# RWKV-6 recurrence and a gated Fourier convolution on one core: states by ScalarE in pieces, merged VectorE sums, a new order

## The chip, the cores and the metric

The kernel runs on one core of a Trainium2 chip. A core has TensorE (PE; its weight loads are listed as PEld), VectorE (DVE), ScalarE (ACT), GpSimd (POOL), and SyncE (SP), whose queue issues the DMAs here. The metric is the device time of one execution in microseconds (us); less is better.

## The reference

Four sequences of 768 steps pass through eight heads of 48 columns with a decaying state, and the result through a gated circular convolution along the sequence.

```python
# r, k, v, w: (4, 8, 768, 48); u: (8, 48)
for t in range(S):
    cur = einsum('bhd,bhe->bhde', u[None] * kt, vt)
    y[:, :, t] = einsum('bhd,bhde->bhe', rt, state + cur)       # the "bonus" is the part with u
    state = wt[:, :, :, None] * state + einsum('bhd,bhe->bhde', kt, vt)
x = y.transpose(0, 2, 1, 3).reshape(B, S, H * D)                # (4, 768, 384)
proj = x @ w_proj                                               # (384, 3 * 384)
x1, x2, x3 = split(proj, 3, axis=-1)
x2_conv = irfft(rfft(x2, axis=1) * rfft(filter_fft, axis=0), n=S, axis=1)
out = (x1 * x2_conv * x3) @ w_out                               # (4, 768, 384)
```

## The kernel before

**Chunks.** The sequence is cut into chunks of 128 steps: six for each of the four sequences (batches), 24 in all, numbered 0 to 23. The steps of a chunk lie on the partitions, the 8 x 48 columns beside each other. For each chunk, four loads of 192 KB (`ldw`, `ldr`, `ldk`, `ldv`, rings of six buffers) are followed by:

- the logarithm of w (`lw`, ScalarE), its running sums by matmuls with triangular masks (`cs`, `ce`), and exponentials (`en`, `eq`; `enp`, `eqp` in place in PSUM), by which k and r are scaled (`kh`, `q` on GpSimd, `khp`, `qp` on VectorE);
- transposes of q and k (`tqk`, TensorE), copied to SBUF in one piece of 128x1024 (`tT`, seen in the trace as `qkT<-tqk`), scores (`sc`), masked on VectorE (`mt`) or copied and then masked (`ma`, `mm`);
- the state: `kv` adds k'v to the last state, and `S` scales the sum by the chunk's decay and writes it as bf16. The next chunk's `kv` and its `y` need it;
- the bonus: `rk`, `rku`, a row sum `cc`, and its product with v, `vc`. Either a matmul adds it (`yb`, then the copy `xc`), or VectorE does (`y`, then `xn`);
- transposes of the chunk's output (`yt`), copied (`xT`).

**Batches.** When the chunks of a sequence are there, the convolution follows as matrix work. Sums and differences of mirrored chunks (`sa`, `sb`, then `fp`, `fm` for each of two halves q) go through the projection `x2`; copies `ab`; the Fourier matmuls `f` with six slots; products with the filter's transform (`da`, `db`, straight from PSUM) and their sums `pp` for each of three column blocks n; the inverse `i1`, `i2`, a copy `ec`, sum and difference `s`, `d`. The other two projections, `p1` (copied by `x1`) and `p3`, give the gate `g`; `yy` multiplies, `po` projects, `o` copies and `st` stores. The last batch uses half-size steps (`i1h`, `i2h`, `ech`, `sh`, `dh`, `yyh`, `poa`, `pob`). The filter's transform and the Fourier matrices (sines, `sin`) are made at the start.

**Order.** The text `ORDER` lists every operation with its engine (V, A, G, P, S for VectorE, ScalarE, GpSimd, TensorE, SyncE) and, behind @, its PSUM bank. Each engine works through its own entries strictly in that order; between engines, semaphores wait for the data and for free buffers. A GpSimd operation marked with ! also waits for the last VectorE operation ahead of it in the text that belongs to the set `shut`. So a late operation holds up everything behind it on its engine. Copies have one line in a helper (L237 on ScalarE, L238 elsewhere), and are told apart in the trace by their tiles. Rows of L464 are the loads of w, r, k, v, of L367 those of the projection weights.

Of the kernel before, what the change touches and what calls it, by code (L numbers as in the profile page):

```python
# [53 lines left out]
P:yt5@1 P:ce7@5 V:sa4 P:x20.0.1@3 V:khp6 A:xT5 A:eq7 V:sb4 P:tqk6@4 V:sa5 A:ab0.0.1 P:x20.1.1@5
V:sb5 V:fp0.0 A:xT3 S:ldr7 A:v6 V:fm0.1 P:x20.0.0@3 P:x20.1.2@2 V:rku6 V:fm0.0 V:fp0.1 S:ldw8 G:q7!
P:x20.0.2@1 S:ldk7 A:ab0.0.0 S:ldp0 A:ab0.1.2 A:ab0.1.1 V:tT6 A:ab0.0.2 S:ldw10 V:cc6 P:f0.0@3
G:kh7! A:xT4 S:ldk8 P:kv6@2 P:x20.1.0@4 V:da0.0 G:vc6! A:ab0.1.0 A:lw8 P:f0.3@1 A:hb2 V:S6 G:rk7!
P:sc6@8 S:ldr8 P:f0.2@4 P:f0.4@2 A:wc0 P:ce8@3 P:tqk7@0 A:eq8 V:db0.1 A:tT7 S:ldw9 P:f0.5@1 P:cs8@5
V:da0.1 V:da0.2 G:rku7! P:p10.2.1@4 V:mt6 G:pp0.1! P:p10.0.1@3 P:p10.2.0@2 A:x10.2.1 S:ldv7 V:db0.2
# [6 lines left out]
S:ldr10 P:p30.0.1@1 A:lw11 V:S8 V:xn8 S:ldk10 A:en10 P:yt6@4 P:ce11@2 V:d0.1 A:tT9 G:q10! S:ldr11
A:eqp11 A:xT6 S:ldw12 S:ldv9 P:p30.0.0@3 G:kh10! A:lw12 V:g0.0.1 V:cc9 V:g0.0.0 P:yt8@5 P:i10.2@0
P:cs11@1 P:sc9@8 A:xT8 A:en11 P:tqk10@4 G:rk10! V:qp11 A:v9 G:rku10! P:p30.1.0@3 S:ldk11 P:p11.0.0@1
A:tT10 P:p11.1.0@2 G:vc9! G:kh11! P:kv9@5 P:cs12@4 A:x11.0.0 V:mt9 V:g0.1.0 V:d0.2 S:ldv10 A:x11.1.0
P:ce12@3 P:y9@1 P:sc10@8 P:tqk11@2 S:ldv11 S:ldw13 A:v10 V:S9 A:eq12 S:ldr12 P:kv10@3 V:cc10 S:ldk12  # L70
# [12 lines left out]
V:da1.1 P:p31.0.1@1 P:kv13@3 P:tqk14@4 G:vc12! P:ce16@0 S:ldr19 P:yb12@2 V:g1.1.1 V:S13 S:ldk19
P:po0.2@5 P:po0.0@3 A:tT14 V:mt13 P:p31.2.1@4 G:rh14! A:xc12 A:eq16 G:vc13! P:cs16@2 P:sc14@8
P:yt12@0 S:ldv19 V:g1.0.1 V:ch14 V:g1.2.1 A:o0.2 P:yb13@5 A:v14 A:enp16 G:kh15! A:o0.0 A:xc13 V:mt14
V:khp16 G:rk15! P:f1.4@4 G:q15! A:xT12 P:tqk15@1 G:q16! G:vc14! G:rku15! G:rk16! P:yt13@5 A:tT15
P:y14@3 A:lw17 A:xT13 S:ldr21 S:ldw21 P:kv14@0 P:tqk16@2 S:ldw23 V:da1.2 V:xn14 A:tT16 P:f1.5@1
P:po0.5@4 S:ldv20 P:yt14@5 P:po0.1@3 V:S14 V:cc15 P:f1.1@0 V:db1.2 G:rk17! P:sc15@8 A:o0.5 A:xT14
# [6 lines left out]
P:i21.2@1 A:eq18 P:i21.0@0 S:st0.3 A:x12.0.0 V:mt17 V:S16 A:v18 A:lw19 G:vc15! P:yt16@3 P:yb15@4
G:q18! A:ec1.2 G:rku18! P:ce19@1 A:v17 A:ec1.0 A:xc15 S:ldv23 S:ldv22 P:tqk18@2 A:tT18 V:sa16 V:sb16
V:xT16 P:y17@0 P:i21.1@3 A:ec1.1 A:eq19 V:d1.0 V:s1.0 P:i11.2@4 G:vc17! V:xn17 P:yt15@2 P:cs19@5
P:x22.1.1@0 G:kh20! V:cc18 A:xT15 G:q20! P:yt17@1 P:i11.1@3 P:sc18@8 A:enp19 V:d1.2 V:s1.2 V:sb15
P:tqk20@4 V:sa15 A:xT17 P:p12.2.1@2 A:ab2.1.1 A:ma18 G:q19! G:rk19! P:p32.0.1@0 V:khp19 G:rk20!
V:sa17 V:d1.1 V:sb17 A:x12.2.1 A:tT20 V:s1.1 P:x22.0.1@5 P:p12.1.1@1 A:ab2.0.1 P:p32.0.0@3 V:fm2.0  # L100
# [852 lines left out]
```

## Time and profile before

| | |
|---|---|
| median of 3 runs | 151.19 us (150.94 to 152.24) |
| the profiled execution | 150.74 us |
| its span, first to last instruction | 148.9 us |
| granted TensorE clock, mean | 0.951 |
| busy, share of the span | PE 90%, DVE 91%, ACT 88%, POOL 73% |
| instructions | PE 1499, DVE 278, ACT 274, POOL 133 |
| HBM read, written | 22.41 MB, 4.72 MB |

Times within the trace count from the start of the span. 1.84 us of the profiled execution's time lie outside it. A share of busy time is a mean over the whole span; an instruction's duration overlaps with the next one's start by about 0.1 us on ScalarE and VectorE, so that the distance from start to start is shorter than the duration.

### The profile page before, as it was taken

To read this page: it belongs to the slowest core of one execution; us is meant where nothing else is said; L and a number is where in the kernel's file an instruction comes from. 1 tells how busy PE (TensorE), PEld (TensorE's weight loads), DVE (VectorE), ACT (ScalarE), POOL (GpSimd) and SP (SyncE) were. 2 spreads that over 40 slices of the span, in tenths; PEclk is the share of its full clock that TensorE was granted. 3 is DMA by queue.
4 is the path that set the end of the run, shared out by engine and by line. 5 is a ranking of instruction groups with operands and counts; after the bars stand their busy time and mean duration, and the time that the engine had idled before them with its cause. 6 is when DMAs were issued, how large, how long until landed. Compare 5 with 4: busy or idle time off the path is not lost.

```text
span 148.9 us, 4080 instructions
## 1 busy us (share of the span) xinstructions
PE 134.0 (90%) x1499; PEld 89.9 (60%) x1499; DVE 134.8 (91%) x278; ACT 130.7 (88%) x274; POOL 108.8 (73%) x133
## 2 busy tenths in 40 slices
...
GB/s 80 212 278 218 181 210 187 219 188 243 178 258 201 263 203 183 217 167 214 227 232 200 222 204 194 198 168 219 229 186 0 4 173 254 0 0 53 314 210 170
...
## 3 DMA queue, kind: packets, MB, share of 16 engines
...
q8 instruction: 11, 0.18, 0.5%
...
HBM read 22.41 MB, written 4.72 MB: 182 GB/s over the span
## 4 chain that ended last, share of the span: by engine, by line
PE 68%; DMA 12%; SPq 5%; POOL 4%; DVE 4%; issue 3%; ACT 1%; ACTq 0%; DVEq 0%; POOLq 0%
PE p L688 14%; PE po L852 8%; PE i L773 6%; PE x L719 6%; PE tqk L561 6%; DMA filt<-in_moe_filter_fft_dram 5%; SPq L464 5%; PE sc L574 4%; DMA ldv<-in_v_dram 4%; DMA ldk<-in_k_dram 3%; PE f L739 3%; PE y L627 2%; PE yt L650 2%; PE cs L474 2%; PE kv L602 2%
## 5 line engine op out<-in xcount | busy, mean ns | idle before, releaser
L535 POOL TENSOR_TENSOR rk<-ldr,ldk 128x384 bf16<-128x384 f32 x23 | 23.0, 1003 | 11.1 <-DMA ldr<-in_r_dram 5.6
L688 PE MATMUL p<-xT,wproj 128*128 128x384 bf16 x144 | 28.8, 326 | 0.0
L555 POOL TENSOR_TENSOR vc<-v,cc 128x384 bf16<-128x384 bf16 x24 | 19.9, 831 | 10.5 <-PE sc L574 3.1
L581 DVE TENSOR_TENSOR mt<-sc,mask_excl 128x1024 bf16<-128x1024 f32 x21 | 25.4, 1210 | 0.1
L237 ACT ACTIVATE qkT<-tqk 128x1024 bf16<-128x1024 bf16 x22 | 22.7, 1031 | 0.7 <-PE tqk L561 0.5
L532 POOL TENSOR_TENSOR qk<-ldr,eq 128x384 bf16<-128x384 f32 x20 | 20.1, 1007 | 3.3 <-DVE rku L538 1.8
L561 PE MATMUL tqk<-ident,qk 128*128 128x128 bf16 x192 | 16.2, 228 | 2.6 <-POOL qk L532 1.8
L688 PEld LDWEIGHTS <-wproj 128*128 128x128 bf16 x144 | 13.0, 97 | 7.4 <-ACT wproj L237 0.3
L561 PEld LDWEIGHTS <-qk 128*128 128x128 bf16 x192 | 12.7, 102 | 5.5 <-POOL qk L532 2.2
L470 ACT ACTIVATE lg<-ldw 128x384 bf16<-128x384 f32 x24 | 12.6, 532 | 2.8 <-DMA ldw<-in_w_dram 2.8
L852 PE MATMUL po<-wout,y 128*128 128x384 bf16 x72 | 14.4, 326 | 0.0
L237 ACT ACTIVATE x<-p 128x384 bf16<-128x384 f32 x24 | 11.7, 505 | 1.5 <-PE p L688 1.5
L237 ACT ACTIVATE ab<-x 128x384 bf16<-128x384 f32 x24 | 11.7, 501 | 1.1 <-PE x L719 0.8
L538 POOL TENSOR_TENSOR rku<-rk,u_bc 128x384 bf16<-128x384 bf16 x13 | 11.8, 913 | 0.4
L541 DVE TENSOR_REDUCE cc<-rku 128x8 f32<-128x384 bf16 x22 | 11.7, 537 | 0.0
L499 ACT ACTIVATE eq<-ce 128x392 f32<-128x392 f32 (+1 forms) x21 | 10.6, 514 | 0.6 <-PE ce L486 0.3
L764 DVE TENSOR_TENSOR UB<-f,T 128x768 bf16<-128x768 f32 x12 | 11.1, 943 | 0.0
L237 ACT ACTIVATE v<-ldv 128x384 bf16<-128x384 f32 x20 | 10.8, 548 | 0.3 <-DMA ldv<-in_v_dram 0.2
L237 ACT ACTIVATE xT<-yt 128x384 bf16<-128x384 bf16 x22 | 10.8, 503 | 0.2
L610 DVE TENSOR_TENSOR S<-kv,eq 128x384 bf16<-128x384 f32 x20 | 10.9, 543 | 0.0
L528 POOL TENSOR_TENSOR qk<-ldk,en 128x384 bf16<-128x384 f32 x10 | 10.0, 1003 | 0.8 <-DMA ldk<-in_k_dram 0.8
L761 DVE TENSOR_TENSOR UA<-f,T 128x768 bf16<-128x768 f32 x11 | 10.3, 943 | 0.1
...
## 6 DMA issues: line engine op xcount, KB each, us to landing
...
```

The costliest lines, as they stand in the source:

```text
L237: return nc.scalar.activation(out=o, in_=i, func=AF.Copy)
L470: nc.scalar.activation(out=lg_b[c % 3][:, :, 0:D], in_=ld["w"][c % LD], func=AF.Ln)
L532: return two(e).tensor_mul(qk_b[c % 3][:, 0, :, 0:D], ld["r"][c % LD], eq)
L535: return two(e).tensor_mul(rk_b[c % 2], ld["r"][c % LD], ld["k"][c % LD])
L538: return two(e).tensor_mul(rku_b[c % 2], rk_b[c % 2], u_bc)
L541: nc.vector.tensor_reduce(out=cc_b[c % 3], in_=rku_b[c % 2], axis=AX.X, op=ALU.add)
L555: return two(e).tensor_mul(vc_b[c % 3], v_b[c % 4], cc_b[c % 3].to_broadcast([L, H, D]))
L561: nc.tensor.transpose(p[:, x, j, :], qk_b[c % 3][:, x, 2 * j:2 * j + 2, :], ident)
L581: nc.vector.tensor_mul(mt_b[c % 3], bank_of[f"sc{c}"].rearrange("p q j t -> p (q j) t"), dataclasses.replace(m[:, :], ap=[m[:, :].ap[0], [ ...
L688: nc.tensor.matmul(p, wproj[:, n, cb, fb * L:(fb + 1) * L], xT_b[b % 2][:, NT * hf:NT * hf + NT, cb, :], start=(cb == 0), stop=(cb == CB - 1),
L764: nc.vector.tensor_mul(UB[:, n], twice(bank_of[f"f.{b}.{2 * n + 1}"][:, :]), t2(n, 1))
L852: nc.tensor.matmul(p, y_b[0][:, cb, ti * L:(ti + 1) * L], wout[:, cb, :], start=(cb == FIRST[0]), stop=(cb == FIRST[-1]),)
```

## The change

The state `S` gets a second form on ScalarE: eight activations with a scale column in place of one VectorE product. It is used for chunks 0, 4, 7, 8, 9, 10, 19, 21 and 22. The bonus products `vc` of chunks 0 and 7 move from GpSimd to VectorE, and chunks 5, 12 and 19 get `xn` on VectorE in place of the bonus matmul and the copy `xc`. The tiles of three rings become one tile each, so that one VectorE instruction does the work of two or three: `fpm`, `fmm` (both halves), `ppm` (three blocks), `yym` (three blocks). Part of the last product is cut in quarters (`yyq`). The halved row sum (`rh`, `ch`) goes. The sines are made first, in four separate steps with one table load, ahead of the table for logarithms and exponentials. `hm`, `um` and `uw` prepare a mask whose result the new order doesn't use. The whole `ORDER` is written anew: many copies and products change engine (on ScalarE fewer `v`, `xT`, `xc`; on GpSimd fewer `rku`, `pp`; on VectorE fewer `khp`, more `xT`), and the loads come in another sequence. The other new functions of the diff stand unused.

The part of `ORDER` around chunk 8, before and after:

```
-A:x10.1.0 P:sc7@8 P:ce9@5 V:db0.0 G:q8! P:tqk8@2 G:v7! V:cc7 V:pp0.0 V:pp0.2 A:eq9 P:p10.1.1@1
-P:kv7@4 P:cs9@5 A:tT8 P:i20.0@3 P:i10.0@2 V:rku8 V:mt7 S:ldp2 V:S7 A:x10.1.1 A:ec0.0 A:en9 A:x10.0.0
-S:ldr9 P:ce10@1 P:i20.2@3 A:wc2 A:ec0.2 S:ldk9 P:sc8@8 V:cc8 V:d0.0 V:s0.0 G:vc7! P:i20.1@4
...
+A:xT6 A:tT7 A:v7 V:db0.1 G:wc0! G:kh8! G:q8! P:p10.0.1@2 P:f0.1@5 A:hb2 S:ldr9 P:p10.1.0@4 P:tqk8@3
+A:x10.0.1 P:f0.4@1 P:p10.2.0@2 P:sc7@8 V:db0.0 P:kv7@5 S:ldk9 S:ldv8 S:ldp2 A:tT8 A:x10.1.0
+A:x10.2.0 G:rku7! P:ce9@3 V:da0.1 G:rk8! P:cs9@4 A:S7 V:da0.2 P:p10.1.1@1 P:p10.0.0@2 A:v8 P:ce10@5
+S:ldw11 V:cc7 P:kv8@0 V:ppm0 V:vc7 A:eq9 P:i20.1@3 V:rku8 A:en9 A:x10.0.0 A:x10.1.1 A:wc2 V:mt7
+P:i20.0@4 P:p10.2.1@2 P:yb7@1 G:kh9! A:eq10 V:x10.2.1 P:sc8@8 A:S8 G:q9! P:p30.2.0@2 A:ec0.0 S:ldw13
```

The loads at the start, and the stretch with the late states:

```
-S:ldw1 S:ldu S:ldw0 S:ldr0 S:ldk0 S:ldk1 S:ldw2 S:ldr1 S:ldfilt S:ldv0 S:ldw3 S:ldr2 ... S:ldw7 S:ldv5 S:ldp1 S:ldk6 ...
+S:ldk1 S:ldw1 S:ldu S:ldw3 S:ldw0 S:ldr1 S:ldv1 S:ldr0 S:ldw2 S:ldk0 S:ldfilt S:ldv0 ... S:ldr6 S:ldk6 S:ldp1 S:ldw7 ...
-A:xT19 A:tT23 A:v22 V:cc22 P:sc22@8 P:po1.0@2 V:mt22 P:po1.5@1 P:yt20@0 P:po1.4@4 P:kv22@5 V:da2.2
-P:sc23@8 V:S22 A:v23 A:o1.5 ...
+V:xT18 V:cc21 P:po1.5@2 P:tqk23@1 V:da2.0 A:tT23 P:sc22@8 P:f2.2@4 A:o1.5 A:xT20 G:rk23! P:kv21@3
+V:rku22 A:S21 G:rku23! V:mt22 G:v23! P:f2.4@0 P:po1.4@1 ... A:v22 P:po1.0@3 V:cc22 P:kv22@2
+V:da2.2 A:x13.1.0 A:X2.2 P:p13.0.0@5 P:y21@4 V:mt23 A:S22 A:o1.4 V:ua2.1 P:p33.0.0@0 A:o1.0 G:vc22!
+A:gc3.0.0 P:y23@2 ...
```

The code:

```diff
@@ op_S
         ph = eq_b[c % 3][:, C:].rearrange("p (a b) -> p a b", b=2)
+        if e == "A":
+            for j in range(HP):
+                for i in (0, 1):
+                    nc.scalar.activation(
+                        out=S_b[nth(c)][:, j, i], in_=bank_of[f"kv{c}"][:, j, i], func=AF.Copy,
+                        scale=ph[:, j, i:i + 1],
+                    )
+            return
         nc.vector.tensor_mul(
             S_b[nth(c)], bank_of[f"kv{c}"], ph.to_broadcast([L, HP, 2, D])
         )
@@ tiles
-    sd_b = ring("sd", 2, [L, NT, CB, L], BF16)
+    sd = consts.tile([L, 2, NT, CB, L], BF16)
-    fo_b = ring("fo", 2, [L, 2, CB, L], BF16)
+    fo = consts.tile([L, 2, 2, CB, L], BF16)
-    SD_b = ring("SD", 3, [L, S], BF16)
+    SD = consts.tile([L, CB, S], BF16)
@@ merged sums and products
+    def op_fpm(e, b):
+        return two(e).tensor_add(fo[:, :, 0], sd[:, :, 0], sd[:, :, 2])
+    def op_fmm(e, b):
+        return two(e).tensor_sub(fo[:, :, 1], sd[:, :, 0], sd[:, :, 2])
+    def op_ppm(e, b):
+        return two(e).tensor_add(P_b[b % 2], UA, UB)
+    def op_yym(e, b):
+        return two(e).tensor_mul(y_b[0], SD, g_b[b % 2])
+    def op_yyq(e, b, cb, a, pt):
+        sl = slice(HALF * a + QUART * pt, HALF * a + QUART * pt + QUART)
+        return two(e).tensor_mul(y_b[0][:, cb, sl], SD[:, cb, sl], g_b[b % 2][:, cb, sl])
@@ the sines
-    def op_sin(e, k_):
-        for ti in range(NT):
-            nc.scalar.activation(out=F[:, ti, :], ..., func=AF.Sin, ...)
-        nc.scalar.activation(out=rot, in_=rang, func=AF.Sin, scale=TWO_PI / (2 * S))
-        nc.scalar.preload_act_table_set("natural_log_exp_and_others")
+    def op_tS(e, k_):
+        nc.scalar.preload_act_table(AF.Sin)
+    def op_sn(e, ti):
+        nc.scalar.activation(out=F[:, ti, :], ..., func=AF.Sin, ...)
+    def op_sr(e, k_):
+        nc.scalar.activation(out=rot, in_=rang, func=AF.Sin, scale=TWO_PI / (2 * S))
```

More of the change, by code (lines that the diff above doesn't have):

```diff
@@ L54 @@
[L54 to L59, printed above, removed]
@@ L66 @@
[L66 to L70, printed above, removed]
@@ L83 @@
[L83 to L88, printed above, removed]
@@ L95 @@
[L95 to L100, printed above, removed]
@@ L107 @@
-P:cs23@4 A:xT18 P:tqk21@0 A:o1.2 V:xn20 V:cc21 A:en23 V:S20 P:x22.0.0@5 P:f2.1@3 G:q22! P:ce23@4
-A:tT21 G:kh22! V:db2.0 G:kh23! G:v21! A:eqp23 P:f2.5@1 V:qp23 A:ab2.0.0 V:db2.2 P:yb19@2 P:sc21@8
-A:xc19 A:ma21 P:f2.0@5 P:tqk22@2 V:da2.0 A:tT22 G:rku22! P:yt19@4 P:f2.4@3 P:kv21@1 P:tqk23@0 V:S21
-A:xT19 A:tT23 A:v22 V:cc22 P:sc22@8 P:po1.0@2 V:mt22 P:po1.5@1 P:yt20@0 P:po1.4@4 P:kv22@5 V:da2.2
-P:sc23@8 V:S22 A:v23 A:o1.5 G:vc21! G:rk23! G:rku23! G:mm21! G:pp2.2! A:xT20 A:o1.0 A:o1.4 P:f2.2@1
-P:y22@3 P:p13.1.0@5 V:mt23 A:x13.1.0 V:cc23 P:y21@4 P:p13.2.0@2 A:x13.2.0 P:p33.0.0@5 P:y23@0
@@ L113 @@
-A:gc3.0.0 G:vc23! G:vc22! P:p13.0.0@2 V:xn21 V:da2.1 P:p33.1.0@5 V:xn23 V:pp2.0 P:yt23@0 V:pp2.1
-P:yt21@1 P:p33.2.0@4 V:gm2.1.1 V:xn22 A:gc3.1.0 A:x13.0.0 A:xT23 P:i12.0@5 P:i22.2@2 V:g3.2.0 V:sb21
-A:ec2.2 P:yt22@3 V:sa21 P:i22.0@0 G:sa23! G:sb23! A:ec2.0 V:sa22 V:sb22 V:fp3.0 P:i22.1@4 V:fm3.1
-A:ec2.1 A:xT22 P:i12.2@2 P:i12.1@0 P:x23.1.2@4 P:x23.1.1@3 V:d2.2 V:s2.0 A:xT21 V:s2.1 V:d2.0
-G:gm2.2.1! G:fp3.1! P:x23.0.0@1 V:s2.2 A:ab3.1.2 P:p13.1.1@4 P:x23.1.0@5 G:fm3.0! A:ab3.0.0 V:d2.1
-V:yy2.1 P:x23.0.1@2 V:yy2.2 P:x23.0.2@0 A:ab3.1.1 A:ab3.1.0 A:ab3.0.1 V:gm2.0.1 A:ab3.0.2 V:yy2.0
@@ new lines @@
+S:ldw11 V:cc7 P:kv8@0 V:ppm0 V:vc7 A:eq9 P:i20.1@3 V:rku8 A:en9 A:x10.0.0 A:x10.1.1 A:wc2 V:mt7
+P:i20.0@4 P:p10.2.1@2 P:yb7@1 G:kh9! A:eq10 V:x10.2.1 P:sc8@8 A:S8 G:q9! P:p30.2.0@2 A:ec0.0 S:ldw13
+V:ec0.1 S:ldk10 P:i10.1@3 P:p30.1.0@0 S:ldr10 V:cc8 G:rk9! G:vc8! P:tqk9@4 V:mt8 A:lw11 P:y8@5
+S:ldv11 V:g0.1.0 A:xc7 V:g0.2.0 A:tT9 S:ldv9 S:ldw12 V:xn8 V:d0.1 P:i10.0@1 P:yt7@0 P:i20.2@2
+P:yt8@5 A:xT7 V:d0.0 A:ec0.2 A:v11 P:i10.2@4 P:p30.0.1@0 P:cs11@2 V:s0.0 V:s0.1 V:d0.2 A:lw13
+V:g0.0.1 A:xT8 P:sc9@8 P:ce11@3 A:en11 A:eqp11 A:lw12 S:ldr11 P:p30.0.0@1 G:kh10! G:q10! G:rku9!
@@ new lines @@
+V:rku22 A:S21 G:rku23! V:mt22 G:v23! P:f2.4@0 P:po1.4@1 S:st1.5 S:st1.3 G:vc21! P:sc23@8 P:p13.1.0@5
+S:st0.0 S:st0.1 V:cc23 G:mm21! S:st1.1 G:vc23! A:v22 S:st0.2 S:st0.5 P:po1.0@3 V:cc22 P:kv22@2
+V:da2.2 A:x13.1.0 A:X2.2 P:p13.0.0@5 P:y21@4 V:mt23 A:S22 A:o1.4 V:ua2.1 P:p33.0.0@0 A:o1.0 G:vc22!
+A:gc3.0.0 P:y23@2 V:xn21 P:p33.1.0@1 V:xn23 P:p13.2.0@4 A:gc3.1.0 P:yt23@2 P:yt21@0 A:x13.2.0
+P:y22@1 V:ppm2 V:xn22 P:p33.2.0@3 V:sb21 P:i22.1@4 G:gm2.1.1! P:yt22@1 A:xT23 A:x13.0.0 P:i12.1@5
+A:gc3.2.0 V:sa23 V:sa22 V:sb22 G:sb23! V:sa21 A:xT22 P:i22.0@2 A:ec2.0 P:i22.2@3 A:ec2.1 P:i12.0@1
@@ new lines @@
+P:i12.2@2 V:gm2.2.1 V:fpm3 A:xT21 A:ic2.0 V:fmm3 V:gm2.0.1 G:dg2.0! A:ec2.2 P:x23.1.1@4 P:x23.0.0@0
+V:s2.1 A:ab3.1.1 A:ab3.0.0 V:s2.0 P:x23.0.1@3 V:s2.2 P:x23.1.0@4 A:ab3.1.0 V:d2.2 P:x23.1.2@0
+P:x23.0.2@2 V:d2.1 A:ab3.0.1 A:ab3.0.2 P:p13.2.1@4 P:f3.0@3 P:f3.1@2 A:ab3.1.2 V:yym2 A:X3.0
+P:f3.4@0 P:f3.5@5 P:f3.3@3 P:f3.2@1 A:X3.5 A:x13.2.1 P:po2.2@5 G:ua3.0! A:o2.2 V:db3.0 V:da3.2
+P:po2.3@4 P:p13.0.1@0 P:po2.1@5 V:ub3.2 V:db3.1 V:da3.1 A:x13.0.1 P:po2.4@3 G:pp3.2! A:o2.1
+P:po2.0@0 A:o2.0 A:o2.3 V:pp3.0 V:pp3.1 P:p13.1.1@1 P:p33.2.1@5 V:gm3.0.0 V:g3.2.1 V:gm3.2.0
@@ new lines @@
+V:gm3.1.0 P:i2h3.2.0@0 P:i2h3.1.0@4 P:i1h3.1.0@2 A:x13.1.1 P:i1h3.2.0@1 S:st2.0 S:st1.0 A:o2.4
+S:st1.4 S:st2.2 A:ech3.2.0 P:i2h3.0.1@3 P:i1h3.0.1@0 A:ech3.1.0 P:i2h3.0.0@4 V:dh3.2.0 V:sh3.2.0
+A:ech3.0.1 P:i2h3.2.1@5 A:ech3.0.0 S:st1.2 S:st2.4 P:i1h3.0.0@1 V:dh3.0.1 P:i1h3.2.1@3 G:yyh3.2.0!
+V:sh3.0.0 V:dh3.0.0 A:ech3.2.1 P:po2.5@4 G:yyh3.0.0! P:p33.0.1@5 P:p33.1.1@1 A:o2.5 V:dh3.1.0
+V:sh3.1.0 S:st2.1 P:poa3.2@4 S:st2.5 S:st2.3 V:dh3.2.1 P:i2h3.1.1@2 V:yyh3.1.0 V:sh3.2.1 P:pob3.2
+P:poa3.0@3 V:sh3.0.1 P:poa3.1@0 V:g3.0.1 V:g3.1.1 P:pob3.0 A:o3.2 A:ech3.1.1 S:st3.2 G:yyh3.2.1!
@@ L325, in op_uv, with op_hm, op_um, op_uw @@
         copy(e, u_bc.rearrange("p h d -> p (h d)"), bank_of["us"])
+    def op_hm(e, k_):
+        nc.gpsimd.memset(hm, 1.0)
+        for lo, m in ((0, 1), (D - 1, -1)):
+            nc.gpsimd.affine_select(
+                out=hm, in_=hm, pattern=[[m * L, CB], [-m * D, H]], base=lo,
+                channel_multiplier=m, compare_op=ALU.is_ge, fill=0.0,
+            )
+    def op_um(e, k_, bank):
+        p = ps("um", bank, (L, CB, H))
+        for cb in range(CB):
+            nc.tensor.matmul(
+                p[:, cb, :], u_top[:, cb * L:(cb + 1) * L], mask_incl[:, 0:H],
+                start=True, stop=True,
+            )
+    def op_uw(e, k_):
+        nc.vector.tensor_mul(uh, bank_of["um"], hm)
     def op_ang(e, ti):
@@ L541, in op_cc, with op_rt, op_rT, op_cu @@
         nc.vector.tensor_reduce(out=cc_b[c % 3], in_=rku_b[c % 2], axis=AX.X, op=ALU.add)
-    def op_rh(e, c):
-        x = rku_b[c % 2]
-        return two(e).tensor_add(rh_b[c % 2], x[:, :, 0:D // 2], x[:, :, D // 2:])
-    def op_ch(e, c):
-        nc.vector.tensor_reduce(out=cc_b[c % 3], in_=rh_b[c % 2], axis=AX.X, op=ALU.add)
+    def op_rt(e, c, bank):
+        p = ps(f"rt{c}", bank, (L, CB, L), BF16)
+        f = rk_b[c % 2].rearrange("p h d -> p (h d)")
+        for cb in range(CB):
+            nc.tensor.transpose(p[:, cb, :], f[:, cb * L:(cb + 1) * L], ident)
+    def op_rT(e, c):
+        copy(e, rT_b[c % 2], bank_of[f"rt{c}"])
+    def op_cu(e, c, bank):
+        p = ps(f"cu{c}", bank, (L, H))
+        for cb in range(CB):
+            nc.tensor.matmul(
+                p, rT_b[c % 2][:, cb, :], uh[:, cb, :], start=(cb == 0), stop=(cb == CB - 1)
+            )
+    def op_cv(e, c):
+        copy(e, cc_b[c % 3], bank_of[f"cu{c}"])
     def op_v(e, c):
@@ L645, in op_xc, with op_xr, op_xg @@
         copy(e, xn_b[c % 3], bank_of[f"y{c}"].rearrange("p h d -> p (h d)"))
+    def op_xr(e, c):
+        op_xc(e, c)
+    def op_xg(e, c):
+        x = xn_b[c % 3]
+        return two(e).tensor_add(x, x, vc_b[c % 3].rearrange("p h d -> p (h d)"))
     def op_yt(e, c, bank):
@@ L706, in op_g, with op_gg @@
         )
+    def op_gg(e, b, fb, hf):
+        nc.vector.tensor_mul(
+            g_b[b % 2][:, fb, halves[hf]], bank_of[f"p3.{b}.{fb}.{hf}"],
+            bank_of[f"p1.{b}.{fb}.{hf}"],
+        )
     def op_gc(e, b, fb, hf):
@@ L806, in op_yy @@
     def op_yy(e, b, cb):
[L807 removed]
+        return two(e).tensor_mul(y_b[0][:, cb, :], SD[:, cb, :], g_b[b % 2][:, cb, :])
     def half(name, bank, b, cb, a, slots):
```

175 lines of the change are left out of this document (101 added, 74 removed).

## The prediction

> **What bounds the kernel now.** I read the page's head first, then busy time by stage (columns: PE, PEld, DVE, ACT, POOL busy with counts, clock, DMA share, GB/s), cut at two copies of the transposed q and k (`qkT`) by ScalarE: those of chunks 8 and 23.
>
> ```profile
> PE 134.0 (90%) x1499; PEld 89.9 (60%) x1499; DVE 134.8 (91%) x278; ACT 130.7 (88%) x274; POOL 108.8 (73%) x133
> ```
>
> ```profile
> 50.37 1.02 ACT L237 ACTIVATE qkT<-tqk 128x1024 bf16<-128x1024 bf16 x1 [0.35 <-PE tqk L561]
> ...
> 117.16 1.07 ACT L237 ACTIVATE qkT<-tqk 128x1024 bf16<-128x1024 bf16 x1
> ```
>
> ```profile
> 0.00:50.37 50.37, 39.54 (x450) 26.77 (x451) 42.02 (x95) 44.36 (x88) 33.00 (x51) 0.86 0.95 209
> 50.37:117.16 66.79, 66.79 (x816) 45.40 (x815) 66.71 (x129) 66.14 (x141) 57.16 (x65) 1.00 0.93 187
> 117.16:148.90 31.74, 27.69 (x242) 17.73 (x236) 26.05 (x56) 20.21 (x47) 18.61 (x19) 0.98 0.37 138
> ```
>
> The reader is to see three stages. In the head, to 50.37 us, no engine is full and the DMA engines are (0.95). In the middle, 66.79 us, TensorE, VectorE and ScalarE are full together: ScalarE shows 0.65 us of idleness (66.79 - 66.14). In the tail only TensorE is nearly full; ScalarE is idle for 11.5 us. The 12% that its share of 88% leaves free lie in head and tail; in the middle it has no room. The chain that ended last agrees:
>
> ```profile
> 48.93 0.97 POOL qk L532
> 49.94 0.40 PE tqk L561 x4
> 50.34 0.49 PE p L688 x3
> ...
> 142.53 1.69 PE po L852 x9
> ```
>
> From 49.94 us it is TensorE without a break to 144.22 us, and what let it start there is GpSimd's product for chunk 8. So the end is: when the middle starts, plus whatever TensorE and the engines that feed it in a fixed order need from there. An engine that is full beside TensorE becomes the bound by whatever is added to it.
>
> **The change part by part.** *States on ScalarE.* `S` is one VectorE product with a broadcast; for nine chunks (0, 4, 7, 8, 9, 10, 19, 21, 22) it becomes eight activations of 128x48, each with a scale column read from memory. What counts in a full engine is the distance from start to start, not the duration:
>
> ```profile
> 84.49 0.54 DVE L610 TENSOR_TENSOR S<-kv,eq 128x384 bf16<-128x384 f32 x1
> 84.95 0.53 DVE L541 TENSOR_REDUCE cc<-rku 128x8 f32<-128x384 bf16 x1
> ```
>
> ```profile
> 17.88 0.48 ACT L237 ACTIVATE m_b<-mtr 128x384 bf16<-128x384 bf16 x1
> 18.25 0.58 ACT L434 ACTIVATE E<-hf,rot 128x384 f32<-128x384 f32 x1
> 18.71 0.50 ACT L506 ACTIVATE cs<-cs 128x384 f32<-128x384 f32 x1
> ...
> 31.94 0.51 ACT L237 ACTIVATE v<-ldv 128x384 bf16<-128x384 f32 x1
> 32.35 0.51 ACT L470 ACTIVATE lg<-ldw 128x384 bf16<-128x384 f32 x1
> 32.77 0.17 ACT L513 ACTIVATE eq<-ce 128x8 f32<-128x8 f32 x1
> 32.83 1.02 ACT L237 ACTIVATE qkT<-tqk 128x1024 bf16<-128x1024 bf16 x1
> ```
>
> ```profile
> L237 ACT ACTIVATE E<-i2h 128x192 f32<-128x192 f32 x6 | 1.8, 330 | 1.0 <-PE i2h L813 0.9
> ```
>
> VectorE gives up 0.46 us a state (84.49 to 84.95). On ScalarE a copy of 384 from PSUM comes every 0.37 us (17.88 to 18.25), one from SBUF every 0.41 (31.94 to 32.35), an activation of 8 columns every 0.06 (32.77 to 32.83): 0.31/376 = 0.82 ns a column, so 48 columns take 0.09. The one with a scale column takes 0.46 (18.25 to 18.71), 0.09 more than without. A piece is then 0.18 us and a state 8 x 0.18 = 1.47 us. No row shows such pieces in a row. Bounds: 0.09 each, 0.74 a state, if the column's reading is hidden behind the piece before; and no overlap at all, 0.20 (between 0.17 for 8 columns and 0.33 for 192) plus 0.08 (0.58 against 0.50) = 0.28, 2.2 a state. I take 1.47, since the nearest row in kind, the scaled one, pays its 0.09 with a neighbour on both sides. Behind each state in ScalarE's queue stand copies that TensorE needs (`ec0.0` and `tT9` soon behind `S8`), so the surplus is handed on.
>
> The Trainium skill ("ScalarE: Activation LUTs", What ACT_TABLE_LOAD costs) gives 186 ns + 0.833 ns a column, 93 ns more for each [128,1] operand, and an overlap of 93 ns. By that an estimate is 0.23 us a piece, 1.81 us a state, and 1.7 us more for five states than I count; the trace agrees on the 93 ns and undercuts the rest for PSUM sources (0.06 us against 0.10 for 8 columns).
>
> *ScalarE in the middle.* I compare the two orders' lists from `A:tT8` to `A:tT23`. Gone: `ec0.1 en10 xT6 xc12 xT14 xT18 xc19`, 7 x 0.37 = 2.59, and `v9 v18`, 2 x 0.41 = 0.82. New there: `x10.1.0 x10.2.0 eq9`, 3 x 0.37 = 1.12, and the states 7, 8, 9, 10 and 19, 5 x 1.47 = 7.35. Net +5.05 us on an engine with 0.65 us of visible idleness. Some waiting also hides between instructions: summed at their own distances, the 140 activations of this stretch make an estimate of 64.1 us of the 66.79. If all waiting went, the stage would grow by 5.05 - 2.7 = 2.4 us; if none, by 5.05. I take the middle, **+3.7**.
>
> *The tail.* Between the copies for chunk 23 and the write of state 22 the new order has, on ScalarE, `o1.5 xT20 S21 v22 x13.1.0 X2.2 S22`: 0.9 for the copy itself, 5 x 0.37 to 0.41 and 2 x 1.47, together 5.7 us.
>
> ```profile
> 119.63 0.54 DVE L610 TENSOR_TENSOR S<-kv,eq 128x384 bf16<-128x384 f32 x1
> ```
>
> Before, that state was written 3.0 us after 117.16. `y23`, the last state product, comes 2.7 us later; TensorE has `p13` and `p33` products of 0.49 us to run meanwhile, and the three bonus matmuls that became additions (`xn` for `xc`, chunks 5, 12, 19) save it 3 x 0.16. Bounds 0 and +2.7; I take **+0.4**, nearer to nothing because those products are there.
>
> *The head.* What released TensorE at 49.94 was a queue on GpSimd:
>
> ```profile
> 42.62 1.00 POOL L528 TENSOR_TENSOR qk<-ldk,en 128x384 bf16<-128x384 f32 x1 [0.80 <-DMA ldk<-in_k_dram]
> ...
> 45.45 0.92 POOL L538 TENSOR_TENSOR rku<-rk,u_bc 128x384 bf16<-128x384 bf16 x1
> 46.33 1.64 POOL L767 TENSOR_TENSOR P<-UA,UB 128x768 bf16<-128x768 bf16 x1
> 47.92 1.01 POOL L535 TENSOR_TENSOR rk<-ldr,ldk 128x384 bf16<-128x384 f32 x1
> 48.88 1.01 POOL L532 TENSOR_TENSOR qk<-ldr,eq 128x384 bf16<-128x384 f32 x1
> ```
>
> ```profile
> 38.35 1.26 SPq L367 DMA_DIRECT2D o<-in_moe_w_proj_dram  x1
> ...
> 40.25 0.52 SPq L464 DMA_DIRECT2D ldk<-in_k_dram  x1
> ```
>
> ```profile
> L238 POOL CAST wproj<-o 128x1152 bf16<-128x1152 f32 x1 | 1.1, 1144 | 0.0
> ```
>
> The `P` of 1.64 us leaves GpSimd (`pp0.1` joins a VectorE sum), `rku7` (0.92) moves behind `q8`, but `wc0` (1.14) and `kh8` (1.00) come ahead of it: -0.4. On SyncE's queue the load of `k8` has 192 KB more ahead of it, and that of the weights `p0` 576 KB, at 209 GB/s 0.9 and 2.8 us later (`p0` was issued at 38.35, so its cast is possible only near 47 to 48 us, ahead of `kh8` on GpSimd). So -0.4 and +0.9 are the ends, and I take **0**. One table load of 1.28 us is saved by running the sines first; the first logarithms then come some 4 us later, and the filter's load has two more loads (1.8 us) ahead: both lie in a stretch that waits for DMA, cost nothing there, and would cost up to those amounts if chunk 8 hung on them.
>
> *Off the path*, with what hides them.
>
> ```profile
> L767 DVE TENSOR_TENSOR P<-UA,UB 128x768 bf16<-128x768 bf16 x9 | 5.1, 608 | 0.0
> ...
> L671 DVE TENSOR_TENSOR fo<-sd 128x384 bf16<-128x384 bf16 x7 | 2.5, 367 | 0.0
> ```
>
> Twice the columns cost 0.61 us where two instructions cost 0.73, so each instruction that a merger (`ppm`, `yym`, `fpm`, `fmm`) saves is worth about 0.1 us. With 9 x 0.46 less for states, and with what VectorE takes over (two `vc` and some sums of GpSimd's, four `xT`, three `xn`), my estimate for all its lists is -1.7 us, for GpSimd -4.7, for TensorE -0.5. As long as ScalarE is last, none shows; it would if the pieces were cheap. The merged products wait for all three thirds before the first output product can start, at most 2 x 0.46 us, behind other TensorE work. Quarters in the last product shorten the end by less than 0.2 us.
>
> **Sum.** 0 + 3.7 + 0.4 = +4.1 us on the profiled execution's 150.74 us (its span 148.9 and 1.84 around it): **154.8 us**. The median of the runs shown is 151.19, 0.45 above that execution; I add nothing for it.
>
> **The rivals.** *(a) The loads win, faster.* Place: SyncE's queue ahead of chunk 6.
>
> ```profile
> 30.81 0.88 SPq L367 DMA_DIRECT2D o<-in_moe_w_proj_dram  x1
> 31.79 0.43 SPq L464 DMA_DIRECT2D ldk<-in_k_dram  x1
> ```
>
> `k6` was issued behind the weights `p1`; now it is ahead of them and of other loads, 768 KB or 3.7 us earlier, and the DMA engines, not ScalarE, set the head. If everything up to chunk 8 follows, the middle begins 3.7 us earlier; with +2.4 in the middle that is 149.4, with the states hidden altogether 147.0; I take 148.4. It decides from a `qkT` of chunk 8 that starts before 46.3 us (50.37 - 4.1). For it: ScalarE is idle for 6 us of the head. Against it: `k8` and `p0` come later, not earlier.
>
> *(b) The pieces are cheap, no change.* At 0.74 us a state the middle gets 5.05 - 5 x 0.73 = +1.4, less the idleness 0.65, and TensorE's -0.5: +0.3, 151.0. This is also the case if the change doesn't do what it says, because the pieces run where ScalarE waits. For it: ScalarE's hidden waiting. Against it: the scaled row.
>
> *(c) The pieces are dearer, or the slower state holds up the next `kv`, much slower.* At 2.2 us a state, 5 x 0.73 more: +7.8, 158.5.
>
> **How the numbers follow.** About 1% is what a measurement of this kernel tells from no change. Forecast 0.51, with its own range of 153.0 to 156.5; (a) 0.27; (b) 0.16; (c) 0.06. So slower 0.57, same 0.16, faster 0.27. The range runs from 148.0, which leaves out the better third of (a), to 157.2, which leaves out most of (c) and a little of the forecast.
>
> **What would show it.** Right: 72 activations that write `S`, some 0.18 us apart; eleven `S` left on VectorE; from the `qkT` of chunk 8 to that of chunk 23 some 70.5 us instead of 66.79, ScalarE without gaps, VectorE with some, TensorE waiting there for ScalarE's copies; the `qkT` of chunk 8 within a microsecond of 50.4. Wrong: pieces 0.1 us apart; or the `qkT` of chunk 8 before 46.3; or a middle that stays at 66.8 with TensorE full, in which case ScalarE had more hidden waiting than I count.

## The result, and the profile after

| | before | changed |
|---|---|---|
| median of 4 runs, us | 151.56 (150.94 to 152.24) | 157.06 (156.52 to 158.35) |
| profiled execution, us | 150.74 | 156.52 |
| its span, us | 148.9 | 154.8 |

The median of before has one run more than the table ahead of the prediction. The ratio is 1.0374, 95% interval 1.0293 to 1.0455: slower by 5.5 us, above the forecast of 154.8 by 1.7 us (profiled execution) or 2.3 (median), and at the upper end of its range: 157.06 us was measured, the ratio times the median before is 157.2, and the range ends at 157.2. Here and below the ratios leave out executions that fell in a slower state, while the medians in us are of all.

The page's busy time of the changed kernel, beside which before's 130.7 us of ScalarE is to be held:

```profile
PE 134.8 (87%) x1499; PEld 89.2 (58%) x1499; DVE 136.5 (88%) x270; ACT 138.2 (89%) x336; POOL 104.3 (67%) x131
```

Its groups by form show how the two kinds of state differ (busy us, mean ns of one | idle us before):

```profile
L648 ACT ACTIVATE S<-kv,eq 128x48 bf16<-128x48 f32 x72 | 15.0, 354 | 0.4 <-PE kv L637 0.2
...
L653 DVE TENSOR_TENSOR S<-kv,eq 128x384 bf16<-128x384 f32 x11 | 6.0, 545 | 0.0
```

72 pieces and eleven products, as the change says. A piece lasts 354 ns, but what counts is the distance of the starts. ScalarE's timeline around chunk 8, in the changed kernel:

```profile
51.13 0.50 ACT L240 ACTIVATE x<-p 128x384 bf16<-128x384 f32 x1
51.51 1.66 ACT L648 ACTIVATE S<-kv,eq 128x48 bf16<-128x48 f32 x8
52.97 0.60 ACT L240 ACTIVATE v<-ldv 128x384 bf16<-128x384 f32 x1
53.38 0.58 ACT L522 ACTIVATE eq<-ce 128x392 f32<-128x392 f32 x1
53.76 0.58 ACT L515 ACTIVATE en<-cs 128x384 f32<-128x384 f32 x1
54.13 0.97 ACT L240 ACTIVATE x<-p 128x384 bf16<-128x384 f32 x2
54.88 1.28 ACT L240 ACTIVATE wproj<-o 128x1152 bf16<-128x1152 f32 x1
55.93 0.61 ACT L522 ACTIVATE eq<-ce 128x392 f32<-128x392 f32 x1
56.31 1.77 ACT L648 ACTIVATE S<-kv,eq 128x48 bf16<-128x48 f32 x8
57.77 0.69 ACT L240 ACTIVATE E<-i 128x384 f32<-128x384 f32 x1
58.15 0.72 ACT L493 ACTIVATE lg<-ldw 128x384 bf16<-128x384 f32 x1
58.56 0.69 ACT L240 ACTIVATE xn<-y 128x384 bf16<-128x384 f32 x1
59.26 1.02 ACT L240 ACTIVATE qkT<-tqk 128x1024 bf16<-128x1024 bf16 x1
60.29 0.49 ACT L240 ACTIVATE xT<-yt 128x384 bf16<-128x384 bf16 x1
```

Eight pieces begin at 51.51 and the next instruction at 52.97: 1.46 us, 0.18 a piece. The second state takes the same (56.31 to 57.77). The copies and exponentials of 384 columns behind it stand start to start at 0.37 to 0.41, without a gap until 59.26.

The three stages, cut at the same two copies of `qkT` (columns as in the prediction: PE, PEld, DVE, ACT, POOL, clock, DMA share, GB/s):

```profile
0.00:49.84 49.84, 36.64 (x431) 25.05 (x432) 40.34 (x93) 43.31 (x97) 32.77 (x53) 0.93 0.98 208
49.84:121.82 71.98, 69.86 (x831) 46.70 (x831) 69.70 (x123) 71.43 (x175) 57.71 (x65) 1.00 0.85 176
121.82:154.80 32.98, 28.31 (x243) 17.43 (x240) 26.45 (x56) 23.50 (x66) 13.84 (x15) 0.99 0.37 132
```

Against 50.37, 66.79 and 31.74 us before: head -0.5, middle +5.2, tail +1.2. In the middle ScalarE alone is full now (71.43 of 71.98); TensorE and VectorE, full before, each have 2 us free. What TensorE waits for in the middle are five things, by its timeline:

```profile
53.21 0.32 PE L503 MATMUL ce<-lg,mask_excl 128*128 128x384 bf16 x1 [0.40 <-ACT S L648]
...
58.13 0.65 PE L744 MATMUL p<-xT,wproj 128*128 128x384 bf16 x3 [0.55 <-ACT S L648]
58.61 0.61 PE L596 MATMUL tqk<-ident,qk 128*128 128x128 bf16 x8
...
66.22 1.14 PE L744 MATMUL p<-xT,wproj 128*128 128x384 bf16 x6 [0.40 <-ACT S L648]
...
71.54 0.32 PE L503 MATMUL ce<-lg,mask_excl 128*128 128x384 bf16 x1 [0.49 <-ACT S L648]
...
116.10 0.32 PE L503 MATMUL ce<-lg,mask_excl 128*128 128x384 bf16 x1 [0.27 <-ACT S L648]
```

Together they are 2.1 us, which is all the time that TensorE is idle there (71.98 - 69.86), and there is one for each of the five states. The waiting matmuls do not read `S`. In `ORDER` each is the next to write into the PSUM bank of that state's `kv` (`ce10` behind `kv7@5`, `p30.1.0` behind `kv8@0`, `p11.1.0` behind `kv9@5`, `ce13` behind `kv10@0`, `ce23` behind `kv19@2`), and the kernel frees that bank only when the state has been made from it. Waits for copies of `qkT`, 3.4 us in this kernel, all lie in the head. The end of the chain that ended last shows the tail's two late states in it:

```profile
123.61 1.53 ACT S L648 x8
125.14 0.41 ACT v L240
125.55 0.38 ACT x L240
125.93 0.29 ACT X L240
126.22 0.05 issue
126.27 1.65 ACT S L648 x8
127.92 0.04 issue
127.96 0.33 PE y L665 x4
128.29 0.20 PE y L670 x8
```

Before, that chain was TensorE alone from 49.94 us on. Here TensorE takes over only at 127.96, once state 22 is written.

### The profile page after: what moved, and what is told of

It is laid out like the page before. It is cut to its first block, busy times and chain, and to the rows that moved or that the text cites. A ratio compares the mean times of both kernels' runs of the same rounds, so it can differ in the third digit from the quotient of the medians.

```text
span 154.8 us, 4130 instructions
## 1 busy us (share of the span) xinstructions
PE 134.8 (87%) x1499; PEld 89.2 (58%) x1499; DVE 136.5 (88%) x270; ACT 138.2 (89%) x336; POOL 104.3 (67%) x131
## 5 line engine op out<-in xcount | busy, mean ns | idle before, releaser
L590 POOL TENSOR_TENSOR vc<-v,cc 128x384 bf16<-128x384 bf16 x22 | 18.1, 829 | 9.7 <-DVE cc L564 4.0
L240 ACT ACTIVATE qkT<-tqk 128x1024 bf16<-128x1024 bf16 x23 | 24.4, 1074 | 0.2
L648 ACT ACTIVATE S<-kv,eq 128x48 bf16<-128x48 f32 x72 | 15.0, 354 | 0.4 <-PE kv L637 0.2
L596 PE MATMUL tqk<-ident,qk 128*128 128x128 bf16 x192 | 14.7, 219 | 0.5 <-ACT eq L522 0.4
L493 ACT ACTIVATE lg<-ldw 128x384 bf16<-128x384 f32 x24 | 14.0, 582 | 0.9 <-DMA ldw<-in_w_dram 0.9
L551 POOL TENSOR_TENSOR qk<-ldk,en 128x384 bf16<-128x384 f32 x12 | 12.0, 1000 | 3.6 <-ACT en L515 3.2
L609 PE MATMUL sc<-qkT 48*128 48x128 bf16 x192 | 9.7, 222 | 3.6 <-ACT qkT L240 3.4
L838 PE MATMUL i<-m_b,P 128*128 128x384 bf16 x54 | 10.6, 326 | 0.0
L609 PEld LDWEIGHTS <-qkT 48*128 48x128 bf16 x192 | 5.7, 95 | 8.4 <-ACT qkT L240 4.4
L760 DVE TENSOR_TENSOR g<-p,x 128x384 bf16<-128x384 f32 x17 | 9.2, 549 | 1.2 <-ACT lg L493 0.6
```

Source lines behind the costliest of these rows:

```text
L240: return nc.scalar.activation(out=o, in_=i, func=AF.Copy)
L493: nc.scalar.activation(out=lg_b[c % 3][:, :, 0:D], in_=ld["w"][c % LD], func=AF.Ln)
L590: return two(e).tensor_mul(vc_b[c % 3], v_b[c % 4], cc_b[c % 3].to_broadcast([L, H, D]))
L596: nc.tensor.transpose(p[:, x, j, :], qk_b[c % 3][:, x, 2 * j:2 * j + 2, :], ident)
L609: nc.tensor.matmul(p[:, par, j, :], t[p0:p0 + D, 1, j, :], t[p0:p0 + D, 0, j, :], start=True, stop=True,)
L648: nc.scalar.activation(out=S_b[nth(c)][:, j, i], in_=bank_of[f"kv{c}"][:, j, i], func=AF.Copy, scale=ph[:, j, i:i + 1],)
```

## The experiments

The question was what the surplus is made of: the price of the pieces, where they stand, or the rest of the new order. Theory 1 is the prediction's: ScalarE is the bound by the pieces' price. Theory 2 was that the order costs the time whatever engine makes the states. All ratios are to the kernel before, run on the same chip beside them.

**All nine states back on VectorE**, at the places that they have in the new order.

```diff
-A:S0 A:S4 A:S7 A:S8 A:S9 A:S10 A:S19 A:S21 A:S22
+V:S0 V:S4 V:S7 V:S8 V:S9 V:S10 V:S19 V:S21 V:S22
```

> The changed kernel with all nine states back on VectorE, at the same places of the order. Theory 1, the pieces on ScalarE are the cause: five states of 1.47 us leave ScalarE's middle (7.35 us), two leave the stretch behind the last copy of q and k, so the stretch from the qkT of chunk 8 to that of chunk 23 falls from 71.98 to 66 to 68 us and the time to 149.5 to 152 us. Theory 2, the new order (loads, merged sums, what VectorE took over) is slow and the pieces only fill it: the stretch stays over 70 us and the time over 155 us.

Measured 158.22 us, ratio 1.0518 (1.047 to 1.0567): worse than on ScalarE. By itself this looked like theory 2. The view of the waits of this kernel says why VectorE did not make use of its room:

```profile
DVE S L653 <- PE kv L637: 3.0, 4, 1.1
```

The places were chosen for ScalarE; on VectorE's list four of them (the states 7, 9, 10 and 21) come before their `kv` is there, and all that is behind them waits 3.0 us, 2.5 of it in the middle.

**The five middle states alone, and the two late ones alone.**

```diff
-A:S7 A:S8 A:S9 A:S10 A:S19
+V:S7 V:S8 V:S9 V:S10 V:S19
```

> Of the nine, only the states 7, 8, 9, 10 and 19 go back to VectorE; 0, 4, 21 and 22 stay on ScalarE. Theory 1: the stretch from chunk 8 to chunk 23 falls by 4 to 6 us as in the kernel with all nine back, the tail keeps its 2 us: 151 to 153 us. Theory 2: no change, 156 to 158 us.

Measured 158.52 us, 1.0538 (1.0456 to 1.0621). The middle is as long as with all nine on VectorE (73.31 us in both), and VectorE waits 2.4 us for `kv` at the same three places.

```diff
-A:S21 A:S22
+V:S21 V:S22
```

> Only the states 21 and 22 go back to VectorE. Theory 1: the middle stays at some 72 us; state 22 is written 2 to 3 us earlier and the tail gives back what it lost, 2 us: 154 to 155.5 us. If the tail was hidden by other matrix work, as the prediction had it (0.4 us): 156.5 us. Theory 2: no change.

Measured 157.2 us, 1.0447 (1.0393 to 1.05). The middle stays at 71.92 us and the tail at 33.3, so the two late states cost as much on VectorE at these places: VectorE stands 0.8 us waiting for `kv21` (state 21 begins at 123.00), the masking behind it comes late, and TensorE waits 1.0 us for it (`sc` at 124.75). What theory 1 expected of these three kernels was missed for two reasons: the places, and that I had taken VectorE for an engine with room because ScalarE was the fuller one.

**The pieces without their scale column.** The count, the order and the tiles stay; only the operand that makes a piece 0.18 instead of 0.09 goes.

```diff
-                        scale=ph[:, j, i:i + 1],
```

> All nine states stay on ScalarE in eight pieces, but without the scale column (the decay is left out of these nine states). Separates the column's cost from the number of pieces. If the column costs its 0.09 us in each piece: pieces 0.09 us apart in place of 0.184, the middle 3.7 us shorter, the tail 1.5: 151.5 to 152.5 us. If a piece costs a fixed 0.18 us whatever it reads: no change, 156 to 158 us.

Measured 151.5 us, 1.0053 (1.0014 to 1.0092). ScalarE's timeline and the middle stage of this kernel:

```profile
51.16 0.95 ACT L648 ACTIVATE S<-kv 128x48 bf16<-128x48 f32 x8
51.88 0.64 ACT L240 ACTIVATE v<-ldv 128x384 bf16<-128x384 f32 x1
```

```profile
49.51:118.11 68.60, 68.60 (x831) 46.43 (x831) 68.36 (x123) 67.98 (x174) 57.45 (x65) 1.00 0.90 185
```

A state now takes 0.72 us (51.16 to 51.88), and 5 us of the span are gone (154.8 to 149.9). TensorE is full again (68.60 of 68.60). No wait of TensorE is listed in the middle any more. So theory 1 holds in its main point: the price of the pieces is the loss, and the rest of the new order, merged sums included, leaves a kernel within a per cent of the one before. The middle is still 1.8 us longer than before's 66.79, with TensorE full: 831 matmuls stand in it where there were 816, and 431 in the head where there were 450.

**A state in one ScalarE copy** of 128x384, 0.37 us, to see whether cheaper still gains more.

```diff
-            for j in range(HP):
-                for i in (0, 1):
-                    nc.scalar.activation(...)
+            copy(e, S_b[nth(c)], bank_of[f"kv{c}"])
```

> The changed kernel with each of the nine states as one ScalarE copy of 128x384 (the decay is left out of these nine states): 0.37 us in place of 1.47. ScalarE then has 5 x 1.10 = 5.5 us less between chunks 8 and 23 than in the changed kernel, 1.9 less than with pieces without a column. If ScalarE is still the only bound: 149.5 to 150.5 us. If TensorE and VectorE are the bound from there, as in the kernel before: 150.8 to 152 us, no shorter than with pieces without a column.

Measured 151.74 us, 1.0042 (0.9998 to 1.0086). The middle stage:

```profile
48.89:117.47 68.58, 68.58 (x831) 46.40 (x831) 68.37 (x123) 66.19 (x139) 57.45 (x65) 1.00 0.90 185
```

ScalarE has 1.8 us less to do than without the column (66.19 against 67.98), and the stage does not move by more than 0.02 us. TensorE sets it. Below 0.72 us a state nothing is to be had from ScalarE in this order.

**Four pieces of 96 columns**, each scaled by one column.

```diff
-                for i in (0, 1):
-                    nc.scalar.activation(out=S_b[nth(c)][:, j, i], ..., scale=ph[:, j, i:i + 1])
+                nc.scalar.activation(out=S_b[nth(c)][:, j], ..., scale=ph[:, j, 0:1])
```

> The changed kernel with each of the nine states in four pieces of 128x96 in place of eight of 128x48, with the scale column of the first head of each pair (half of each state is scaled wrongly). By the distances so far a piece of 96 with a column takes 0.06 + 0.08 + 0.09 = 0.23 us, a state 0.92. If ScalarE binds from a price of about 0.75 us a state on, and what is above it is added in full: 5 x 0.17 = 0.9 us over the kernel with pieces without a column, 152.3 us. If the loss starts only near the full price of 1.47: 151.5 us. If it is proportional from nothing: 154 us.

Measured 151.98 us, 1.0084 (1.0019 to 1.0149). The timeline of this kernel:

```profile
51.10 1.05 ACT L647 ACTIVATE S<-kv,eq 128x96 bf16<-128x96 f32 x4
51.99 0.57 ACT L240 ACTIVATE v<-ldv 128x384 bf16<-128x384 f32 x1
```

0.89 us a state, and the middle grows by 0.3 to 68.94 (one trace each; two other pairs with the same list there agree within 0.06 us, 71.98 and 71.92, 73.31 and 73.31). The times of whole executions do not tell these two kernels apart (ratios 1.0084 and 1.0053, with intervals that overlap), and 151.98 us lies between the first two expectations. From 0.89 to 1.47 it is 0.58 a state, 2.9 for the five of the middle, and the middle grows by 3.0 (68.94 to 71.98): above some 0.7 to 0.9 us a state the excess is paid.

How it is paid has two readings, and no run separates them. One is ScalarE's list, which gets longer by the excess. The other is the bank: TensorE was ready for `ce10` 1.30 us after state 7 began (at 52.81, in the changed kernel), and a state lasts 1.66 us from its first start to its last end there, 1.05 in four pieces and 0.95 without the column. State 7 itself was not late: it began at 51.51, and on VectorE in the first experiment, with a head of the same length, its `kv` let it begin at 51.41.

**The states on VectorE, three of them later**, where their `kv` is ready.

```diff
-A:S7 ... A:S9 ... A:S10          (the other six to V: at their places)
+V:cc7 V:S7 ... V:cc10 V:S9 ... V:cc11 V:S10
```

> The changed kernel with all nine states on VectorE, the states 7, 9 and 10 one to three VectorE operations later in the order than in the first experiment, where VectorE stood 2.5 us waiting for kv ahead of them. Theory 1, extended: VectorE is as full as ScalarE, and the first experiment lost by VectorE's 2.3 us of added states and by waiting at these places: 155.5 to 157 us. If only the places cost: 153 to 155 us. If the waiting is harmless: 158 us as in the first.

Measured 155.62 us, 1.0288 (1.0202 to 1.0373). The waiting in the middle is gone (0.5 us is left in the tail, for `kv21`), and what is left is price:

```profile
49.63:120.25 70.62, 69.66 (x831) 46.62 (x831) 70.54 (x128) 64.46 (x135) 57.50 (x65) 1.00 0.87 180
```

VectorE is full (70.54 of 70.62) while ScalarE has 6 us free: the order gave VectorE other work in exchange for its states, so it has no room for them either. Three places on VectorE's list are all that separates this kernel from that of the first experiment (ratios 1.0288 and 1.0518).

**A split of the states between the two**, to pool the room: 8, 10 and 19 on VectorE, the other six on ScalarE.

```diff
-A:S8 ... A:S10 ... A:S19
+V:S8 ... V:cc11 V:S10 ... V:S19
```

> The changed kernel with the states 8, 10 and 19 back on VectorE (10 two VectorE operations later), and 0, 4, 7, 9, 21 and 22 on ScalarE in eight pieces. If each of the two engines adds what it has above its room: ScalarE keeps 2 x 1.47 = 2.9 us between chunks 8 and 23, under the 3.7 at which it did not bind; VectorE gets 3 x 0.46 = 1.4; the late states keep their 1.2: the middle 69.5 to 70.5 us and 153 to 154.5 us, between the kernel with free pieces and either extreme. If only ScalarE mattered: 152 us. If the states cost the same wherever they stand: 156 to 157 us.

Measured 155.93 us, 1.0365 (1.0251 to 1.048): above the 153 to 154.5 of pooled room, and next to the last alternative, that a state costs the same wherever it stands. The middle stage:

```profile
50.28:121.29 71.01, 69.83 (x831) 46.54 (x831) 69.77 (x126) 67.29 (x151) 57.41 (x65) 1.00 0.87 179
```

Now no engine is full over the stage (69.83, 69.77 and 67.29 of 71.01), and it is still 2.4 us longer than with cheap states. The two states that stayed on ScalarE here still hold up TensorE at their banks, as long as when ScalarE was full (0.40 for each of them in the changed kernel):

```profile
53.65 0.32 PE L489 MATMUL ce<-lg,mask_excl 128*128 128x384 bf16 x1 [0.40 <-ACT S L634]
...
66.39 1.14 PE L730 MATMUL p<-xT,wproj 128*128 128x384 bf16 x6 [0.39 <-ACT S L634]
```

That speaks for the reading by the bank for these two waits. Cut once more, at the `qkT` of chunk 13, the stretch with the states 7 to 10 tells how they are paid (us, chunk 8 to chunk 13; the floor is 26.04, with one copy a state):

| kernel | stretch | above the floor | the four states' own price |
|---|---|---|---|
| VectorE, ScalarE's places | 30.47 | 4.43 | 4 x 0.46 on VectorE, and 2.5 of waiting for `kv`: 4.34 |
| changed | 28.80 | 2.76 | 4 x 1.47 on ScalarE, less 4 x 0.74: 2.92 |
| split | 28.16 | 2.12 | 2 x 0.73 on ScalarE and 2 x 0.46 on VectorE: 2.38 |
| VectorE, three later | 27.77 | 1.73 | 4 x 0.46 on VectorE: 1.84 |
| four pieces | 26.36 | 0.32 | 4 x 0.15 on ScalarE: 0.60 |
| without column | 26.06 | 0.02 | 0 |

Each row is within 0.3 us of adding up the excesses, whichever engine bears them; on VectorE the price counts from nothing, since without the nine states it is full there already (68.36 of 68.60 in the run without the column). That reading was made after the runs and fits all of them; placements with the states further apart were not tried.

**The same pieces in the old order.** The kernel before, with the new form of `S` for the nine states and nothing else.

```diff
-V:S0 V:S4 V:S7 V:S8 V:S9 V:S10 V:S19 V:S21 V:S22       (in before's ORDER)
+A:S0 A:S4 A:S7 A:S8 A:S9 A:S10 A:S19 A:S21 A:S22
```

> The kernel before with one part of the change alone: the nine states on ScalarE, eight pieces each, at the places where VectorE had them. Theory 1, ScalarE's surplus is added in full: five states between the copies of chunks 8 and 23, 5 x 1.47 = 7.35 us, less 0.65 of idleness, and 2 us in the tail: 158 to 161 us. Theory 3, the pieces are harmless where the order leaves room and only the new order's places are bad: 151 to 154 us.

Measured 166.07 us, 1.0957 (1.0849 to 1.1064), worse than either theory said. The middle stage (from 52.75, the `qkT` of chunk 8 in this kernel):

```profile
52.75:128.68 75.93, 68.71 (x821) 46.19 (x820) 67.04 (x127) 74.97 (x189) 58.70 (x66) 1.00 0.81 163
```

Head +2.4, middle +9.1, tail +3.5. Here the states are added to ScalarE with nothing taken off. The new order with the same pieces is 5.5 us slower than before, this one 15: two thirds of what the pieces do to the old order does not arise in the new one. By which of its changes, no run tells.

**The merged sums alone**, in the old order (`fpm`, `fmm`, `ppm`, `yym` where their parts stood next to each other, and the undivided row sum).

```diff
-V:fp0.0 V:fp0.1 ... V:fm0.0 V:fm0.1 ... V:pp1.0 V:pp1.1 V:pp1.2 ... V:yy0.0 V:yy0.1 V:yy0.2
+V:fpm0 ... V:fmm0 ... V:ppm1 ... V:yym0
```

> The kernel before with another part alone: the merged sums and products of VectorE (both halves of fp and fm for batches 0 and 2, pp of batch 1, yy of batches 0 to 2), and the row sums of chunks 14 and 17 unhalved. VectorE has some 0.9 us less to do, and the merged results come later than the first of their parts did. If VectorE has a say in the middle: 150 to 151 us; if TensorE alone: 151 to 152 us.

Measured 152.52 us, 1.0062 (1.0015 to 1.011): no gain, a loss of half a per cent if anything. Whether that is the waiting for all thirds stays open. What a merger is worth, start to start, show VectorE's timelines of before (three sums in a row) and of the changed kernel (one `ppm`):

```profile
92.88 1.48 DVE L767 TENSOR_TENSOR P<-UA,UB 128x768 bf16<-128x768 bf16 x3
94.28 0.54 DVE L516 TENSOR_TENSOR qk<-cs,ldk 128x384 bf16<-128x384 f32 x1
```

```profile
97.15 1.35 DVE L833 TENSOR_TENSOR P<-UA,UB 128x2304 bf16<-128x2304 bf16 x1
98.42 0.54 DVE L564 TENSOR_REDUCE cc<-rku 128x8 f32<-128x384 bf16 x1
```

1.27 us for what took 1.40: 0.13 saved, where two instructions less at 0.1 each were counted. So the mergers do relieve VectorE, by a little less than I took, but in the run above nothing of it reached the end.

## Why the prediction was right or wrong

- **The price of a piece: right.** 0.18 us predicted, 0.18 measured; 1.47 a state predicted, 1.46 measured. By the estimate from the Trainium skill ("ScalarE: Activation LUTs", What ACT_TABLE_LOAD costs) it would have been 0.23 and 1.81. Its 93 ns for a [128,1] operand agree with the run without the column (0.18 against 0.09), the rest of its sum comes out 0.04 us a piece too long here.
- **What binds: half right.** "An engine that is full beside TensorE becomes the bound by whatever is added to it." ScalarE is full in the middle, and VectorE and TensorE have gaps. But the surplus was to be handed on by the copies that stand behind each state, with "TensorE waiting there for ScalarE's copies". The waits that the trace lists there are all for the states themselves, to free the banks of their `kv`. The prediction did not have that path.
- **The head: near.** 0 predicted within -0.4 and +0.9, -0.5 measured, just outside. Kernels whose lists are the same up to chunk 8 have heads of 49.84 (changed), 49.86 (late states on VectorE), 50.28 (split) and 50.72 us (middle states on VectorE), so half a microsecond is not to be read. The loads won none of the 3.7 us of rival (a).
- **The middle: undersized, and this is the step that failed**: "If all waiting went, the stage would grow by 5.05 - 2.7 = 2.4 us; if none, by 5.05. I take the middle, **+3.7**." It grew by 5.2. The count of ScalarE's work (+5.05) was right, and none of the waiting gave way: by the same sum of own distances, an estimate again, the changed middle holds 69.1 us of work in 71.98, so 2.9 of waiting where 2.7 was. Seen from TensorE, the 5.2 have two parts. 1.8 are TensorE's own list, as the run without the column shows (68.60 against 66.79); the forecast had TensorE at -0.5. The other 3.4 come with the price of the states, which is 5 x 0.74 = 3.7 above that run's. 2.1 of the 3.4 are the five waits for banks; the other 1.3 lie in TensorE's busy time (69.86 against 68.60, for the same 831 matmuls), and no view says where. Halving between two bounds was no reasoning.
- **Why the waiting stayed** is shown for one gap. ScalarE's copy of `qkT` at 59.26 comes 0.70 us after the start ahead of it, where 0.37 would do. It needs `tqk9`, which TensorE ran only at 58.61, because it had stood 0.55 us ahead of 58.13 for the bank of `kv8`, until state 8 was done. So there a state's own length comes back to ScalarE as waiting. Whether the other gaps are of this kind is not shown.
- **The tail: undersized.** +0.4 predicted within 0 and +2.7, +1.2 measured. State 22 was written 6.1 us after the `qkT` of chunk 23 (121.82 to 127.92), 5.7 predicted. TensorE's timeline there, in the changed kernel:

```profile
125.19 0.65 PE L945 MATMUL po<-wout,y 128*128 128x384 bf16 x3 [0.46 <-ACT S L648]
...
126.01 0.65 PE L744 MATMUL p<-xT,wproj 128*128 128x384 bf16 x3
...
126.87 0.65 PE L744 MATMUL p<-xT,wproj 128*128 128x384 bf16 x3
127.96 0.33 PE L665 MATMUL y<-S,qkT 128*128 128x96 bf16 x4 [0.45 <-ACT S L648]
```

The `p13` and `p33` products (three matmuls each) are there as cover, and end at 127.52; state 22 is later still by 0.45. That is the size of the +0.4 that I took. What the working left out is the wait for state 21 (0.46, ahead of 125.19, where `po1.0` is to go into the bank of `kv21`): I priced only the later of the two. The last 0.3 of the 1.2 are not traced. With cheap states the tail is as before (31.79 without the column, 31.74 before).
- **Profile and median: a term put at nothing.** "I add nothing for it": the median was 0.54 above the profiled execution, as 0.45 before. So the 2.3 us between forecast and median are 1.5 of the middle, 0.8 of the tail and 0.5 of this, less 0.5 of the head.
- **Rival (b), cheap pieces, 151.0**: not what happened, but the run without the column is this rival, at its own 0.74 us a state, and took 151.5. 151.0 plus seven late or middle states at the full 0.73 is 156.1, against 156.52. That its sum fits so well is in part luck: it had +0.3 in the middle, where that run has +1.8, and a head 0.9 shorter makes up for part of it.
- **Off the path: half right.** GpSimd was relieved (108.8 to 104.3 us busy), and that shows nowhere in the end. VectorE's list was to be 1.7 us shorter; its busy time is 1.7 us longer (134.8 to 136.5), and no shorter than before where the same list is not held up (134.8 without the column). So its room for states was less than I thought, as the runs with states on VectorE then showed.

No version here beats the kernel before. The best of the new order, whose states leave out the decay, end about half a per cent behind the old one: TensorE is full in both, and its 68.6 us in the middle, 1.8 more than before, set the pace there.
